# A Fourier mixing layer and an MLP on one core: the second half of a block's first w_out products is issued a step later

## The chip, the core and the metric

The kernel runs on one core of a Trainium2 chip. The core has a matrix engine (TensorE, "PE" in the profile, with its weight loads "PEld"), VectorE ("DVE"), ScalarE ("ACT"), GpSimd ("POOL") and SyncE ("SP", which here issues DMAs). The metric is the time of one execution on the device in microseconds, as the median of several runs.

## The reference

The input x is 8 sequences of 3008 tokens with 256 features. Each sequence is convolved along its tokens with a filter that is given by its spectrum, and the result goes through an MLP with a gated nonlinearity:

```
X = np.fft.rfft(x, axis=1)
F = (filt_r + 1j * filt_i)[None, :, :]
Y = X * F
y = np.fft.irfft(Y, n=x.shape[1], axis=1)      # 8 x 3008 x 256
h = y.reshape(24064, 256) @ w_in               # 24064 x 2048
g = h * (1.0 / (1.0 + np.exp(-beta * h)))
out = g @ w_out                                # 24064 x 256, float32
```

## The kernel before

The Fourier part is done as products with tables: 3008 = 47 * 64, so that a transform is a stage of 47 points (`s1`, L619), a stage of 64 points with the filter (`s23`, L641 to L670: a forward product, a complex multiplication with the filter on VectorE and GpSimd, an inverse product three units later), and a last stage of 47 points (`s4` through `last4`, L544). Between stages the data go through DRAM scratch to change their layout. The first sequence is done in a setup part of its own; the other seven are cut into small units, each with one or a few products and an evacuation, and a table `plan` says at which step of the MLP loop each unit is issued (`place`, L696).

The MLP loop (L812) takes 47 blocks of 512 tokens, and in each block 16 slices `fb` of 128 hidden features: 752 steps. In step s:

- two products of 512 columns (L825) give h for the slice in a PSUM tile `hps` (two buffers), and ScalarE turns it into `gT` (L834, Silu; w_out was divided by beta beforehand), in one of four buffers;
- then come the planned units of this step (L839). Their PSUM tiles are in `fpsum` (three buffers), and are emptied by VectorE or ScalarE;
- then, for the slice of two steps before (`LAG` is 2), four products of 256 columns (L860) add gT times w_out to the block's accumulators, one product for each 128 tokens (`tb`).

A block's accumulators are two PSUM tiles of two 128-token parts each, from `opsum`, which has three buffers (L83, L850). So of a new block's two tiles, the first finds the third buffer free, and the second takes the buffer that the old block's first tile leaves. At the end of a block (`fb` 15, L868) the two tiles are copied to SBUF one after the other by VectorE (`ost`, L109; in the first six blocks the first of the two by ScalarE, L107) and stored. In the last block each 128-token part has a tile of its own, from two pools.

The order on each engine is the order in which the Python code issues instructions: the kernel asks for a manual schedule, and the tile pools only add the waits. TensorE runs its products in this order, and a product that waits holds all behind it.

Of the kernel before, what the change touches and what calls it, by code (L numbers as in the profile page):

```python
# [9 lines left out]
P = 128  # L10
# [27 lines left out]
def kernel(  # L38
# [19 lines left out]
    NFB = FF // P  # L58
# [42 lines left out]
    wout_sb = wpool.tile([P, NFB, D], BF16, name="wout_sb", tag="wout_sb")  # L101
# [3 lines left out]
    def evac(dst, src, on_act, scale=None):  # L105
        if on_act:
            nc.scalar.activation(dst, src, ACT.Copy, scale=1.0 if scale is None else scale)  # L107
        elif scale is None:
            nc.vector.tensor_copy(dst, src)  # L109
        else:  # L110
            nc.vector.tensor_scalar_mul(dst, src, scale)  # L111
# [672 lines left out]
    def store(t0, tn, ost, eng=nc.sync):  # L784
        if t0 >= S:
            eng.dma_start(
                out[t0 : t0 + tn, :].rearrange("(c p) d -> p c d", p=P), ost[:, : tn // P, :]
            )
            return
        for tb in range(tn // P):  # L790
            c0 = t0 + tb * P
            c1 = c0 + P
            while c0 < c1:
                lo = (c0 - t0) % P
                if c0 >= S:
                    nc.sync.dma_start(out[c0:c1, :], ost[lo : lo + c1 - c0, tb, :])
                    break
                g, r = divmod(c0, CLS)
                n = min(c1 - c0, CLS - r)
                nc.sync.dma_start(  # L800
                    AP(
                        out.tensor,
                        out.offset + (r // JC * J + g * JC) * D,
                        [[J * D, n // JC], [D, JC], [1, D]],
                    ),
                    ost[lo : lo + n, tb, :],
                )
                c0 += n
# [3 lines left out]
    for s in range(len(steps) + LAG):  # L812
        if s < len(steps):
            i, fb = steps[s]
            t0 = i * TB
            tn = min(TB, TOK - t0)
            hps = hpsum.tile([P, TB], F32, name="hps", tag="hps")
            pos = t0
            while pos < t0 + tn:
                b, n0 = divmod(pos, S)  # L820
                ln = min(S - n0, t0 + tn - pos)
                if s == 0:
                    ln = min(ln, CLS - n0 % CLS)
                for dc in range(NDC):
                    nc.tensor.matmul(  # L825
                        hps[:, pos - t0 : pos - t0 + ln],
                        lhsT=win_sb[:, dc, fb * P : (fb + 1) * P],
                        rhs=ys[b][:, dc, n0 : n0 + ln],
                        start=(dc == 0),
                        stop=(dc == NDC - 1),  # L830
                    )
                pos += ln
            gT = gpool.tile([P, TB], BF16, name="gT", tag="gT")
            nc.scalar.activation(  # L834
                gT[:, :tn], hps[:, :tn], ACT.Silu, scale=beta_sb[:, fb : fb + 1]
            )
            blk[s] = gT
        if s in plan:
            for go in plan[s]:  # L839
                go()  # L840
        if s >= LAG:
            i, fb = steps[s - LAG]
            t0 = i * TB
            tn = min(TB, TOK - t0)
            nch = tn // P
            gT = blk.pop(s - LAG)

            last = i == NBLK - 1
            if fb == 0 and not last:
                acc = [opsum.tile([P, 2, D], F32, name="acc", tag="acc") for _ in range(2)]  # L850
            elif fb == 0:
                acc = [
                    (fpsum if h % 2 else opsum).tile(
                        [P, 1, D], F32, name="acc", tag="f" if h % 2 else "acc"
                    )
                    for h in range(nch)
                ]
            per = acc[0].shape[1]
            for tb in range(nch):
                nc.tensor.matmul(  # L860
                    acc[tb // per][:, tb % per, :],
                    lhsT=gT[:, tb * P : (tb + 1) * P],
                    rhs=wout_sb[:, fb, :],
                    start=(fb == 0 and tb % per == 0),
                    stop=(fb == NFB - 1),
                    skip_group_check=True,
                )
            if fb == NFB - 1:  # L868
                for h, a in enumerate(acc):
                    if h * per % 2 == 0:  # L870
                        ost = ostp.tile([P, 2, D], F32, name="ost", tag="ost")
                    c = h * per % 2
                    on_act = h == 0 and i < 6 or last and h % 2 == 0
                    evac(ost[:, c : c + per, :], a[:], on_act)
                    eng = nc.scalar if last and h >= 2 else nc.sync
                    store(t0 + h * per * P, per * P, ost[:, c : c + per, :], eng)
# [30 lines left out]
```

## Time and profile before

| | us |
|---|---|
| median of 7 runs | 789.67 (788.96 to 791.22) |
| the profiled execution | 791.28 |
| its span, first to last instruction | 789.5 |
| TensorE busy | 777.2 (98%) |
| ScalarE busy | 597.3 (76%) |
| VectorE busy | 394.1 (50%) |
| w_out products (L860), 3008 | 456.0 |
| w_in products (L825), 1730 | 448.2 |

The share of the TensorE clock that was granted is 0.998 over the span. A row of the order of time gives start, duration, engine, line, operation, the tiles written and read, their shapes, how many instructions were merged, and in brackets how long the engine sat idle before it and what ended that. Products of TensorE overlap: a 256-column product is shown with 273 ns, but the next one starts 109 ns after it, so that four in a row show 0.60 us. A wait between two of them can hide in a longer merged duration.

### The profile page before, as it was taken

What the parts mean: (1) busy time and instruction counts of PE and PEld (TensorE: products, weight loads), DVE (VectorE), ACT (ScalarE), POOL (GpSimd) and SP (SyncE); (2) the same over time, 40 slices, a digit from 0 to 9 for tenths busy, and PEclk for the clock granted to TensorE, in tenths of its full rate; (3) what the DMA queues carried; (4) which work ended last, traced back from release to release, by engine and by line L of the source; (5) the groups of instructions that cost most, each with busy time, mean ns of one, the idle gap of its engine ahead of it and who ended that gap; (6) DMA issues with size and microseconds to landing.
All of it is one profiled execution on the core that took longest, in us unless ns stands there. A gap on an engine that the chain in (4) does not pass through costs nothing.

```text
span 789.5 us, 15550 instructions
## 1 busy us (share of the span) xinstructions
PE 777.2 (98%) x6111; PEld 548.4 (69%) x6111; DVE 394.1 (50%) x645; ACT 597.3 (76%) x922; POOL 144.5 (18%) x143
## 2 busy tenths in 40 slices
PE   8989999999999999999999999999999999999998
PEld 5757667766777667876668766687667776776665
DVE  8837935746537464465534746367452761500101
ACT  6967886886678866788677876778767788677776
POOL 8522500430013200131002310024000340000000
PEclk9999999999999999999999999999999999999999
DMA  9978674516811178012860228412360214110101
GB/s 192 249 171 214 162 205 141 126 67 187 226 35 51 64 201 219 28 67 87 199 180 28 95 94 194 152 51 77 125 205 27 75 67 127 44 38 28 54 27 54
DMA packets 84185, 91.46 MB, mean 116 GB/s; under 512 B 4498, under 2 KB 74276, under 8 KB 83154
## 3 DMA queue, kind: packets, MB, share of 16 engines
q1 hardware_dynamic: 81008, 73.95, 30.3%
q0 software_dynamic: 2816, 16.26, 10.6%
q8 instruction: 48, 0.79, 0.4%
q10 hardware_dynamic: 288, 0.26, 0.1%
q14 instruction: 25, 0.20, 0.1%
HBM read 57.16 MB, written 46.66 MB: 131 GB/s over the span
## 4 chain that ended last, share of the span: by engine, by line
PE 91%; DVE 4%; DMA 2%; issue 2%; ACT 1%; POOL 0%; DVEq 0%; ACTq 0%; POOLq 0%
PE acc L860 41%; PE hps L825 40%; PE ps L619 3%; PE ps L544 3%; PE ps L641 2%; PE ps L667 2%; DVE ost L109 1%; DMA d<-a 1%; DVE qb_t L444 1%; DMA xg<-in_x_dram 1%; DVE pb_t L444 0%; DVE q_t L656 0%; DVE q_t L653 0%; DVE a_t L109 0%; PE pz L536 0%
## 5 line engine op out<-in xcount | busy, mean ns | idle before, releaser
L834 ACT ACTIVATE gT<-hps,beta_sb 128x512 bf16<-128x512 f32 x752 | 516.2, 687 | 176.8 <-PE hps L825 165.6
L860 PE MATMUL acc<-wout_sb,gT 128*128 128x256 bf16 x3008 | 456.0, 273 | 1.2 <-ACT ost L107 0.2
L825 PE MATMUL hps<-y,win_sb 128*128 128x512 bf16 (+8 forms) x1730 | 448.2, 351 | 0.3 <-ACT gT L834 0.3
L860 PEld LDWEIGHTS <-gT 128*128 128x128 bf16 x3008 | 285.7, 98 | 132.7 <-issue 4.6
L825 PEld LDWEIGHTS <-win_sb 128*128 128x128 bf16 x1730 | 165.0, 98 | 24.9 <-issue 0.6
L657 POOL TENSOR_TENSOR v_t<-p_t,q_t 128x512 bf16<-128x512 f32 x84 | 106.7, 1271 | 396.0 <-DVE q_t L656 393.1
L109 DVE COPY ost<-acc 128x512 f32<-128x512 f32 (+1 forms) x88 | 56.3, 678 | 193.6 <-PE acc L860 190.6
L109 DVE CAST a<-ps 96x512 bf16<-96x512 f32 x96 | 65.8, 686 | 90.4 <-PE ps L619 85.3
L111 DVE TENSOR_SCALAR y<-ps 128x376 bf16<-128x376 f32 (+1 forms) x119 | 64.5, 545 | 62.5 <-PE ps L544 62.4
L652 DVE TENSOR_TENSOR p_t<-ps,frr 128x512 f32<-128x512 f32 x84 | 58.1, 692 | 32.0 <-PE ps L641 29.3
L656 DVE TENSOR_TENSOR q_t<-ps,fri 64x512 f32<-64x512 f32 x84 | 58.3, 694 | 1.2
L653 DVE SCALAR_TENSOR_TENSOR q_t<-ps,fri 64x512 f32<-64x512 f32 x84 | 57.4, 684 | 1.1
L544 PEld LDWEIGHTS <-zz 96*128 96x128 bf16 x512 | 35.3, 97 | 31.0 <-issue 2.3
L107 ACT ACTIVATE z<-ps 128x512 bf16<-128x512 f32 x84 | 49.5, 590 | 0.8 <-PE ps L667 0.7
L619 PE MATMUL ps<-xg,t 94*96 94x512 bf16 x112 | 42.2, 382 | 0.0
L544 PE MATMUL ps<-t,zz 96*128 96x94 bf16 x448 | 36.7, 204 | 0.0
L667 PE MATMUL ps<-v_t,t 128*128 128x256 bf16 x168 | 32.1, 273 | 0.6 <-DVE q_t L656 0.6
L641 PE MATMUL ps<-a,t 128*128 128x256 bf16 x168 | 32.1, 273 | 0.0
L118 POOL DMA_DIRECT2D xg<-in_x_dram x22 | 12.1, 552 | 101.6 <-PE acc L860 97.7
L641 PEld LDWEIGHTS <-t 128*128 128x128 bf16 x168 | 15.8, 98 | 14.6
L619 PEld LDWEIGHTS <-t 94*96 94x96 bf16 x112 | 13.8, 123 | 12.1
L667 PEld LDWEIGHTS <-t 128*128 128x128 bf16 x168 | 15.4, 98 | 8.4 <-DVE q_t L656 1.4
(120 smaller groups left out, 195.6 us busy)
## 6 DMA issues: line engine op xcount, KB each, us to landing
out_dram<-ost SPq DMA_DIRECT2D x80, 256.0 KB, 2.1
d<-a SPq DMA_DIRECT2D x28, 384.0 KB, 3.7
a<-d SPq DMA_DIRECT2D x28, 384.0 KB, 5.2
d<-z SPq DMA_DIRECT2D x28, 384.0 KB, 2.3
zz<-d SPq DMA_DIRECT2D x28, 384.0 KB, 6.8
xg<-in_x_dram POOLq DMA_DIRECT2D x6, 1280.0 KB, 10.2
frr<-in_filt_r_dram SPq DMA_DIRECT2D x12, 256.0 KB, 6.8
out_dram<-ost SPq DMA_DIRECT2D x18, 128.0 KB, 2.4
```

What stands on the lines that cost most here:

```text
L109: nc.vector.tensor_copy(dst, src)
L111: nc.vector.tensor_scalar_mul(dst, src, scale)
L544: nc.tensor.matmul(ps[:, e, :NP], lhsT=zz[:, jj + e, dc * P : (dc + 1) * P], rhs=tab[:], start=True, stop=True,)
L619: nc.tensor.matmul(ps[:KP], lhsT=t1[:], rhs=s["x"][:, 2 * i : 2 * i + 2, :], start=True, stop=True)
L641: nc.tensor.matmul(ps[:, e, :], lhsT=t2[:, k0 + e, 3:5, :].rearrange("p c k -> p (c k)"), rhs=s["a2"][g][:, kk + e, :], start=True, stop=True,
L652: nc.vector.tensor_tensor(p_t[:], ps[:], frr[:, ks_, :], ALU.mult)
L656: nc.vector.tensor_tensor(q_t[:M], ps[M:P], fri[M:P, ks_, :], ALU.mult)
L657: nc.gpsimd.tensor_tensor(v_t[:], p_t[:], q_t[:], ALU.add)
L667: nc.tensor.matmul(ps[:, e, :], lhsT=t3[:, k0 + e, :], rhs=v_t[:, e, :], start=True, stop=True)
L825: nc.tensor.matmul(hps[:, pos - t0 : pos - t0 + ln], lhsT=win_sb[:, dc, fb * P : (fb + 1) * P], rhs=ys[b][:, dc, n0 : n0 + ln], start=(dc ...
L834: nc.scalar.activation(gT[:, :tn], hps[:, :tn], ACT.Silu, scale=beta_sb[:, fb : fb + 1])
L860: nc.tensor.matmul(acc[tb // per][:, tb % per, :], lhsT=gT[:, tb * P : (tb + 1) * P], rhs=wout_sb[:, fb, :], start=(fb == 0 and tb % per = ...
```

## The change

The loop over the four products at a step becomes a list of (gT, fb, tb). In a block's first step (`fb` 0) only the first half of the list (the 128-token parts 0 and 1, which go to the first tile) is issued; the second half is kept in `late`. In the next step (`fb` 1) the kept products are put into the middle of the list: parts 0 and 1 of slice 1, then parts 2 and 3 of slice 0, then parts 2 and 3 of slice 1. So at the next step TensorE runs the two L825 products, the planned units, and then six w_out products. All other steps are as before, and each sum is taken in the same order. In the new file the products stand at L867.

```
-            for tb in range(nch):
+
+
+            todo = [(gT, fb, tb) for tb in range(nch)]
+            if fb == 0:
+                todo, late = todo[: nch // 2], todo[nch // 2 :]
+            elif fb == 1:
+                todo[nch // 2 : nch // 2] = late
+            for g_, f_, tb in todo:
                 nc.tensor.matmul(
                     acc[tb // per][:, tb % per, :],
-                    lhsT=gT[:, tb * P : (tb + 1) * P],
-                    rhs=wout_sb[:, fb, :],
-                    start=(fb == 0 and tb % per == 0),
-                    stop=(fb == NFB - 1),
+                    lhsT=g_[:, tb * P : (tb + 1) * P],
+                    rhs=wout_sb[:, f_, :],
+                    start=(f_ == 0 and tb % per == 0),
+                    stop=(f_ == NFB - 1),
                     skip_group_check=True,
                 )
```

## The prediction

> **What bounds the kernel now.** I read the summary of busy time first, then the table of costliest groups, then the table of waits, then the order of time at the places where a block of 512 tokens ends.
>
> ```profile
> PE 777.2 (98%) x6111; PEld 548.4 (69%) x6111; DVE 394.1 (50%) x645; ACT 597.3 (76%) x922; POOL 144.5 (18%) x143
> ...
> L860 PE MATMUL acc<-wout_sb,gT 128*128 128x256 bf16 x3008 | 456.0, 273 | 1.2 <-ACT ost L107 0.2
> ```
>
> TensorE is the bound: 98% busy, and its chain of work is 91% of the span. The change removes no product, so it can only win time in which TensorE waits. By the group's row that is 1.2 us before the w_out products (L860). The table of waits shows more, on the weight loads of the same line:
>
> ```profile
> PEld L860 <- issue: 4.6, 20, 0.4
> ```
>
> Twenty waits, 4.6 us, at most 0.4 us each. The order of time says where they lie. This is block 8's first step:
>
> ```profile
> 180.13 1.27 DVE L109 COPY ost<-acc 128x512 f32<-128x512 f32 x2
> 180.20 0.38 PE L667 MATMUL ps<-v_t,t 128*128 128x256 bf16 x2
> 180.31 0.32 PEld L860 LDWEIGHTS <-gT 128*128 128x128 bf16 x3
> 180.42 0.83 PE L860 MATMUL acc<-wout_sb,gT 128*128 128x256 bf16 x4
> ...
> 180.87 0.10 PEld L860 LDWEIGHTS <-gT 128*128 128x128 bf16 x1 [0.24 <-issue]
> ```
>
> Four L860 products normally show 0.60 us and start 0.109 apart; here they take 0.83. The first two write the free third accumulator buffer. The third writes the buffer that held the old block's first half, which VectorE copies out until 180.13 + 0.68 = 180.81; it starts at 180.87. So 0.23 us is lost, inside what counts as busy.
>
> Here the Trainium skill must be weighed against the row. Perfetto Trace Analysis, "Identifying the Most-Contended Engine", says that TensorE's busy share is a bad measure of headroom, because pipelined products overlap. By the idle column (1.2 us) the change wins at most 0.15%, nothing measurable; by start-to-start times it may win four times that. The stretched 0.83 decides for the second.
>
> **What is removed.** I took the third product's start less the second's, less 0.109, at each of the 47 block starts. From 164 to 642 us the pattern repeats every six blocks: 0, 0.23, 0.28, 0.14, 0.07, 0, five times 0.72 = 3.60 us. The rest of the run has 0.14 once and 0.07 to 0.08 seven times: 0.67. Blocks 3, 4 and 5, where ScalarE copies the first half, have 0.15, 0.18 and 0.40: 0.72. Sum 5.0 us of waits for the old accumulator (the table's 4.6 plus pieces too short for it).
>
> **Where those products go.** In the new order the first step of a block has two L860 products instead of four; the next step's two L825 products follow (0.43 us), then a planned unit of the mixing, if that step has one, two of its own products (0.22), and then the two late ones. They come at least 0.65 us later than before, and the longest wait was 0.40. So all 5.0 us go. Nothing new is loaded or copied: still 64 products a block, each with its weight load; the queues of VectorE, ScalarE, GpSimd and SP keep their order, no DMA moves. The late products read the Silu result gT one step longer; four gT buffers rotate, and the Silu that overwrites one already waits for a later L825 product. If that cover were gone, ScalarE's 0.69 us Silu would slip, behind 0.2 to 0.4 us of its own slack.
>
> **What comes earlier.** Everything between is two products, 0.218 us, earlier against the other engines: L825 of the second step, and that step's unit.
>
> L825 needs a Silu of two steps before. At 180.87 ScalarE runs the first step's Silu, so the one needed ended before 180.46, while L825 would start at 180.42 + 0.22 = 180.64. No wait. The Silu behind it ends at 180.46 + 0.69 = 181.15, before the L825 after next.
>
> The unit is less safe. In twelve blocks (6, 7, 12, 13, 18, 19 and so on to 37, those with the 0 in the pattern) units of the third stage stand in the first and in the second step. Block 7:
>
> ```profile
> 164.38 0.69 ACT L834 ACTIVATE gT<-hps,beta_sb 128x512 bf16<-128x512 f32 x1 [0.18 <-PE hps L825]
> ...
> 164.55 0.60 PE L860 MATMUL acc<-wout_sb,gT 128*128 128x256 bf16 x4
> ...
> 164.96 0.59 ACT L107 ACTIVATE z<-ps 128x512 bf16<-128x512 f32 x1
> ...
> 165.42 0.38 PE L641 MATMUL ps<-a,t 128*128 128x256 bf16 x2
> 165.60 0.14 PEld L667 LDWEIGHTS <-t 128*128 128x128 bf16 x2
> 165.64 0.38 PE L667 MATMUL ps<-v_t,t 128*128 128x256 bf16 x2
> ```
>
> The second L667 unit takes the buffer that ScalarE empties into z: 164.96 + 0.59 = 165.55. Its weight load waits for that and starts at 165.60, just in time for a product at 165.64. Nothing ahead of z changes: Silu and z both depend on products issued before the moved ones. So z still ends at 165.55, while PE arrives at 165.64 - 0.218 = 165.42. What a late weight load costs is shown once in this trace, in block 6:
>
> ```profile
> 149.17 0.38 PE L641 MATMUL ps<-a,t 128*128 128x256 bf16 x2
> ...
> 149.55 0.11 PEld L667 LDWEIGHTS <-t 128*128 128x128 bf16 x2 [0.28 <-ACT z L107]
> 149.55 0.39 PE L667 MATMUL ps<-v_t,t 128*128 128x256 bf16 x2
> 149.67 0.42 PEld L860 LDWEIGHTS <-gT 128*128 128x128 bf16 x4
> 149.78 0.60 PE L860 MATMUL acc<-wout_sb,gT 128*128 128x256 bf16 x4
> ```
>
> The two L641 products should hand over at 149.17 + 0.22 = 149.39; L667 starts at 149.55, 4 ns after its load starts, and the next pair runs 10 ns late. So in block 7: 165.60 + 0.004 - 165.42 + 0.010 = 0.19 us. Eleven blocks times 0.19 is 2.1; block 6, which waits already, gets the whole 0.22 on top: 2.35 us in all.
>
> A rule of the skill speaks against the change just here. TensorE: Matmul & The Clock Gate, "Step-by-step: what each phase is for", lets the engine pull weight loads ahead, but "The MATMULs themselves stay in program order". If later products could pass the waiting one, the new waits would cost 0; by the rule they cost all of their 0.19. The row agrees with the rule: at 149.55 four ready L860 products stood behind L667 and none went ahead. I take the full cost.
>
> One more block: in block 3 the unit after is an L619 product at 98.50 whose buffer VectorE frees at 97.55 + 0.69 = 98.24 (q_t, L656). With the 0.15 us wait gone and two products fewer it would come at 98.13, and can come at 98.24 + 0.05: 0.15 us new, 0.03 of an old wait at 99.61 gone: 0.12.
>
> Lower bound of the new waits: 0, if the buffers were freed earlier, for which nothing speaks. Upper: 98 ns more at each of twelve places, if a product waits for its whole load (an L667 load's own duration): 1.2 us; the nearest row (4 ns at 149.55) is against it.
>
> **Sum.** 5.0 - 2.35 - 0.12 = 2.5 us, 0.32%. The profiled execution: span 789.5 us to 787.0; its own time 791.28 (1.8 outside the span) to 788.8. It stood 1.6 above the median of the runs, 789.67, so the median goes to 787.2.
>
> **Rivals.** (A) The new waits do not come: all 5.0 us won, 784.7 us. For it: the accumulator waits are certain, the L667 ones are shifted by arithmetic. Against: z's end at 165.55 leaves only 0.04 us.
>
> (B) The change doesn't do what it says: the late pair still waits, or every 0.218 us of advance is given back at the next unit, in nearly all blocks. Then 26 saved waits become other waits: 789.7. For it: after the wait is gone VectorE still does two copies (1.27 us) before its next unit. Against: the first units after the starts of blocks 8 and 9 have 2.4 us between their buffer's release and their start.
>
> (C) Slower: ScalarE becomes the bound in the twelve blocks. There a step costs PE 1.31 us (164.12 to 165.42), ScalarE a Silu and a z, at 0.58 + 0.72 between starts. In the shortened step PE asks again after 1.09. If z slips behind the next Silu by its 0.69 us, each place costs 0.19 + 0.69 = 0.88, together 10.6 us: 795.3. It decides above 5.0/12 = 0.42 us a place. For it: ScalarE has only 0.18 us idle there. Against: z stands before the next Silu in its queue, and that Silu's input comes after z has started.
>
> **How the numbers follow.** The sum as worked: 0.75. A: 0.08. B, or half of it: 0.12. C: 0.05. A measurement of this kernel tells about 0.2% (1.6 us) from no change; the seven runs lie 2.3 us apart. Faster by more means below 788.1: the sum's case less some bad luck (0.70) and A (0.08): 0.78. Within: 0.17. Slower: 0.05. The sum's own range is 786.3 to 788.3 (upper bound of the loads: gain 1.3); to hold eight in ten with half of A and of B it is 785.6 to 788.9.
>
> **What the new profile would show.** The first pair of a block's L860 products at 0.38 us and six after the next L825 (0.82 us), no stretched 0.83, no wait "PEld L860 <- issue" beyond the 55 us region. New: twelve waits of L667's loads for ScalarE's z (L107), near 0.19 us of PE time each, one of 0.38 in block 6. Wrong if these are absent (A), if L860 still waits for VectorE (B), or if L825 waits for Silu (C). Also outside my sum: at 55 us PE waits 2.0 us for a copy and the granted clock is 0.52 for 3.4 us, before the first changed wait; if its length differs between executions the median moves by about a microsecond.

## The result and the profile after

The changed kernel takes 786.86 us in the median (14 runs, 786.25 to 787.88), the kernel before 789.56 us (33 runs, 788.43 to 793.19). The ratio is 0.9964, with a 95% interval of 0.9956 to 0.9972: 2.7 us by the medians, 0.36% by the ratio, faster. The forecast was 787.2 us.

The page of the profiled execution, its first part and the row of the w_out products (L867 now):

```profile
span 784.7 us, 15550 instructions
...
PE 774.7 (99%) x6111; PEld 547.9 (70%) x6111; DVE 393.6 (50%) x645; ACT 595.1 (76%) x922; POOL 144.6 (18%) x143
...
L867 PE MATMUL acc<-wout_sb,gT 128*128 128x256 bf16 x3008 | 451.4, 272 | 0.0
```

The number of instructions is the same on every engine. The w_out products show 451.4 us busy where they showed 456.0: the 4.6 us less are mostly waits that had been counted as busy, in stretched merged products (the rest is the half clock near 55 us, told below). This is block 8's start in the order of time:

```profile
177.59 1.27 DVE L109 COPY ost<-acc 128x512 f32<-128x512 f32 x2
177.66 0.38 PE L667 MATMUL ps<-v_t,t 128*128 128x256 bf16 x2
177.77 0.21 PEld L867 LDWEIGHTS <-gT 128*128 128x128 bf16 x2
177.87 0.38 PE L867 MATMUL acc<-wout_sb,gT 128*128 128x256 bf16 x2
...
178.09 0.59 PE L825 MATMUL hps<-y,win_sb 128*128 128x512 bf16 x2
```

After the first pair the next L825 product starts 0.22 us later, the normal hand-over; the 0.83 us product group is gone, though VectorE's copy stands as late against TensorE as before. In the table of waits the twenty "PEld L860 <- issue" are gone (19 of them stood at block starts, one in the half clock near 55 us; a new one of 0.15 us stands in block 3, behind a product that waits there), and these rows are there (waiter, releaser, us in total, times, longest):

```profile
PEld L667 <- ACT z L107: 3.8, 12, 0.5
...
PEld L825 <- issue: 0.6, 1, 0.6
...
PE hps L825 <- ACT gT L834: 0.3, 1, 0.3
```

The kernel before has one wait of this kind, in block 6:

```profile
PEld L667 <- ACT z L107: 0.3, 1, 0.3
```

So eleven waits for ScalarE's z are new and block 6's is longer, and L825 has no waits beyond the single ones that stood before. Block 7's second step:

```profile
162.22 0.59 ACT L107 ACTIVATE z<-ps 128x512 bf16<-128x512 f32 x1
...
162.47 0.38 PE L641 MATMUL ps<-a,t 128*128 128x256 bf16 x2
162.73 0.69 ACT L834 ACTIVATE gT<-hps,beta_sb 128x512 bf16<-128x512 f32 x1
162.87 0.11 PEld L667 LDWEIGHTS <-t 128*128 128x128 bf16 x2 [0.30 <-ACT z L107]
162.87 0.39 PE L667 MATMUL ps<-v_t,t 128*128 128x256 bf16 x2
...
162.99 0.21 PEld L867 LDWEIGHTS <-gT 128*128 128x128 bf16 x2
163.10 0.27 PE L867 MATMUL acc<-wout_sb,gT 128*128 128x256 bf16 x1
```

L667 could have started at 162.47 + 0.22 = 162.69 and starts at 162.87. By start-to-start times it loses 0.186 us here and in each of the other ten blocks of this kind, and 0.385 in block 6, where 0.165 stood before.

The spans of the two profiled executions differ by 4.8 us, more than the medians. Past 60 us the difference is 2.4. The rest lies at 54 to 58 us, before the first changed wait: in both executions TensorE waits there for a PSUM buffer that ScalarE empties into `a`, and ScalarE waits for the DMA that copies an older `a` to DRAM. The kernel before:

```profile
54.21 0.59 ACT L107 ACTIVATE a<-ps 96x512 bf16<-96x512 f32 x1 [2.80 <-DMA d<-a]
...
54.86 0.33 PE L544 MATMUL ps<-t4b,zz 96*128 96x94 bf16 x4 [2.00 <-ACT a L107]
```

And after the change:

```profile
53.50 0.59 ACT L107 ACTIVATE a<-ps 96x512 bf16<-96x512 f32 x1 [2.08 <-DMA d<-a]
...
54.14 0.33 PE L544 MATMUL ps<-t4b,zz 96*128 96x94 bf16 x4 [1.29 <-ACT a L107]
```

By start-to-start times the wait is 2.17 us before and 1.45 after. Before, the granted clock was also halved behind it (the 0.52, third from the right, in this table of a stretch; the second row is the stretch after the change):

```profile
55.00:58.40 3.40, 3.40 (x22) 2.32 (x20) 0.78 (x2) 2.50 (x5) 0.00 (x0) 0.52 0.21 58
```

```profile
53.90:58.00 4.10, 3.86 (x39) 2.94 (x39) 1.95 (x4) 3.62 (x8) 0.00 (x0) 1.00 0.43 123
```

So the medians, not these two spans, measure the change.

### The profile page after: what moved, and what is told of

Its sections match the earlier page's. It is cut to its first block, busy times and chain, and to the rows that moved or that the text cites. A ratio compares the mean times of both kernels' runs of the same rounds, so it can differ in the third digit from the quotient of the medians.

```text
span 784.7 us, 15550 instructions
## 1 busy us (share of the span) xinstructions
PE 774.7 (99%) x6111; PEld 547.9 (70%) x6111; DVE 393.6 (50%) x645; ACT 595.1 (76%) x922; POOL 144.6 (18%) x143
## 4 chain that ended last, share of the span: by engine, by line
PE 94%; DVE 3%; issue 1%; DMA 1%; ACT 1%; DVEq 0%; ACTq 0%
PE acc L867 41%; PE hps L825 41%; PE ps L619 3%; PE ps L544 3%; PE ps L667 3%; PE ps L641 2%; PE pw L187 1%; DVE qb_t L444 1%; DMA d<-a 1%; DVE a_t L109 0%; ACT gT L834 0%; DVE pb_t L444 0%; DVE q_t L656 0%; DVE q_t L653 0%; PE pz L536 0%
## 5 line engine op out<-in xcount | busy, mean ns | idle before, releaser
L867 PE MATMUL acc<-wout_sb,gT 128*128 128x256 bf16 x3008 | 451.4, 272 | 0.0
L825 PE MATMUL hps<-y,win_sb 128*128 128x512 bf16 (+8 forms) x1730 | 447.7, 351 | 0.3 <-ACT gT L834 0.3
L867 PEld LDWEIGHTS <-gT 128*128 128x128 bf16 x3008 | 285.5, 98 | 127.4 <-ACT gT L834 0.2
L825 PEld LDWEIGHTS <-win_sb 128*128 128x128 bf16 x1730 | 165.0, 98 | 24.7 <-issue 0.6
L667 PE MATMUL ps<-v_t,t 128*128 128x256 bf16 x168 | 32.2, 273 | 1.1 <-DVE q_t L656 0.6
L641 PE MATMUL ps<-a,t 128*128 128x256 bf16 x168 | 32.1, 273 | 0.0
L641 PEld LDWEIGHTS <-t 128*128 128x128 bf16 x168 | 15.8, 98 | 14.6
L667 PEld LDWEIGHTS <-t 128*128 128x128 bf16 x168 | 15.1, 98 | 11.0 <-ACT z L107 3.8
```

Of the source, the lines that this page charges most:

```text
L641: nc.tensor.matmul(ps[:, e, :], lhsT=t2[:, k0 + e, 3:5, :].rearrange("p c k -> p (c k)"), rhs=s["a2"][g][:, kk + e, :], start=True, stop=True,
L667: nc.tensor.matmul(ps[:, e, :], lhsT=t3[:, k0 + e, :], rhs=v_t[:, e, :], start=True, stop=True)
L825: nc.tensor.matmul(hps[:, pos - t0 : pos - t0 + ln], lhsT=win_sb[:, dc, fb * P : (fb + 1) * P], rhs=ys[b][:, dc, n0 : n0 + ln], start=(dc ...
L867: nc.tensor.matmul(acc[tb // per][:, tb % per, :], lhsT=g_[:, tb * P : (tb + 1) * P], rhs=wout_sb[:, f_, :], start=(f_ == 0 and tb % per = ...
```

## The experiments

The theory: 5.0 us of waits for the old accumulator go, and about 2.4 us of new waits come, nearly all in the twelve blocks where a third-stage unit (one that contains L667's inverse product) stands in each of the first two steps. Rival 1: the gain is the shorter stretch near 55 us, through block 0's new order. Rival 2: TensorE makes up for the waits for z later, so that they cost nothing.

**The change in the twelve blocks alone** (no accumulator wait stood there):

```
-            if fb == 0:
+            if fb == 0 and i % 6 < 2 and 6 <= i < 38:
                 todo, late = todo[: nch // 2], todo[nch // 2 :]
-            elif fb == 1:
+            elif fb == 1 and i % 6 < 2 and 6 <= i < 38:
                 todo[nch // 2 : nch // 2] = late
```

> The second pair is held back only in the twelve blocks whose second step has a third-stage unit (6, 7, 12, 13, ... 36, 37), none of which had an accumulator wait. Theory (5.0 us of accumulator waits go, 2.3 us of waits for ScalarE's z come): only the cost is left, 11 x 0.186 + 0.22 = 2.3 us, 791.9 us, with twelve waits of L667's weight load for L107 in the trace. Rival 1 (the gain is the shorter stretch near 55 us, where the two profiled executions differ by 2.4 us, moved by block 0's new order): block 0 is as before, so 789.6 us. Rival 2 (the waits for z are made up later and cost nothing): 789.6 us.

Measured: 791.78 us (22 runs) against 789.69 for the kernel before, ratio 1.0026 (1.0017 to 1.0034). The table of waits of this run has both kinds:

```profile
PEld L867 <- issue: 4.3, 19, 0.4
...
PEld L667 <- ACT z L107: 3.8, 12, 0.5
```

This is the cost alone, 2.1 us. Rival 2 falls: the waits are not made up. Rival 1 is at 789.6 as well, and falls with it as an explanation of this run; the next run and the table at the end of this section speak of its gain.

**The change in all blocks but these** (the same two lines with `not (...)`):

> The second pair is held back in all blocks but those twelve. Theory: all 5.0 us of accumulator waits go, of the new waits only block 3's 0.14 us is left: 789.6 - 4.9 = 784.7 us. Rival 1 (the stretch near 55 us): block 0 has the new order, so as the change, 786.9 us. Rival 2 (waits for z cost nothing): as the change, 786.9 us.

Measured: 784.64 us (6 runs), ratio 0.9930 (0.9914 to 0.9946), 5.05 us faster than before. The waits of L667 for z are back to one:

```profile
PEld L667 <- ACT z L107: 0.3, 1, 0.3
```

Gain and cost, measured apart, are -5.05 and +2.09: together -2.96, where the whole change measured -2.7. Block 0 has the new order here and in the change, yet the two differ by 2.2 us, so Rival 1 cannot be the cause of that difference.

**The late pair ahead of the unit.** The pair is issued in the second step directly behind the L825 products, before the planned unit, so that the unit comes no earlier than it did:

```
+        if s >= LAG and steps[s - LAG][1] == 1:
+            w_out(late)
         if s in plan:
             for go in plan[s]:
                 go()
...
             if fb == 0:
                 todo, late = todo[: nch // 2], todo[nch // 2 :]
-            elif fb == 1:
-                todo[nch // 2 : nch // 2] = late
```

(`w_out` holds the loop over the products.)

> The second pair is held back in every block, but issued in the second step ahead of the planned unit instead of behind it, so that the unit comes no earlier than before. It is still 0.43 us (the two L825 products) later than before, and the longest accumulator wait was 0.40. Theory: 5.0 us won and no new wait: 784.6 us. Rival 1: 786.9 us. Rival 2: 786.9 us. A third possibility, that the pair waits again because 0.43 us is too short, would show as L860-type waits for VectorE or ScalarE and end between 784.6 and 786.9.

Measured: 784.00 us (6 runs, 783.52 to 784.88), ratio 0.9921 (0.9905 to 0.9937): the fastest kernel of this study. Block 7's second step in its order of time:

```profile
161.32 0.38 PE L815 MATMUL acc<-wout_sb,gT 128*128 128x256 bf16 x2
...
161.54 0.38 PE L641 MATMUL ps<-a,t 128*128 128x256 bf16 x2
...
161.72 0.14 PEld L667 LDWEIGHTS <-t 128*128 128x128 bf16 x2
161.76 0.38 PE L667 MATMUL ps<-v_t,t 128*128 128x256 bf16 x2
```

L667 follows L641 after the normal 0.22 us. Block 7 had no accumulator wait, but no row "PEld L815 <- issue" is left in the whole table of waits either, so 0.43 us of delay is enough for block 5's 0.40 too. Why it came 0.6 us lower than the sum is not settled; the sum lies at the interval's edge (0.9937 times 789.69 is 784.7). In its profiled execution the wait at 54 us was only 0.03 us, and behind that stretch it gained no more than the sum (table below).

**All four products held back**, which doubles the advance:

```
             if fb == 0:
-                todo, late = todo[: nch // 2], todo[nch // 2 :]
+                todo, late = [], todo
             elif fb == 1:
-                todo[nch // 2 : nch // 2] = late
+                todo = late[: nch // 2] + todo[: nch // 2] + late[nch // 2 :] + todo[nch // 2 :]
```

> All four products of a block's first step are held back to the second, which doubles the advance of what is issued between to 0.436 us. Theory: the twelve waits for z grow by 0.218 each to 0.40, 4.9 us with block 6; block 3's to 0.37; and where no unit stands in the first step (11 blocks) L825 comes 0.43 + 0.87 = 1.30 us after the L825 of two steps before, whose Silu ends after 0.216 + 0.48 + 0.69 = 1.39 and is seen 0.05 later: 0.13 us each, 1.5 us. Sum -5.0 + 4.9 + 0.3 + 1.5 = +1.7: 791.3 us. Rival 1: 786.9 us. Rival 2: 786.9 us, or 788.4 if only the L825 waits count.

Measured: 791.40 us (22 runs), ratio 1.0019 (1.0010 to 1.0028). Slower than before, though every accumulator wait is gone. The waits:

```profile
PEld L667 <- ACT z L107: 6.4, 12, 0.7
...
PEld L825 <- issue: 2.7, 10, 0.6
```

By start-to-start times L667 loses 0.405 us in eleven blocks and 0.602 in block 6, which is the 0.186 of the change plus the 0.218 of two more products. And L825 waits for the Silu of two steps before in 13 blocks, about 0.13 us each; the expectation had counted 11. This is the order of time at such a place, the start of block 40: four L825 products merged, 1.16 us instead of 0.435 + 0.59 = 1.03.

```profile
687.16 1.16 PE L825 MATMUL hps<-y,win_sb 128*128 128x512 bf16 x4
688.15 1.03 PE L867 MATMUL acc<-wout_sb,gT 128*128 128x256 bf16 x8
```

**The units moved away.** The change, with third-stage units never in two steps that follow each other:

```
                 at += (2 - at) % NFB
+            if clear and n and at - last_at < 2:
+                at = last_at + 2
```

> The change, with the third-stage units never in two steps that follow each other: a unit that would stand in a block's second step goes to its third. Theory: the twelve waits for z go, because z has a whole step more; all 5.0 us of accumulator waits are won, block 3's new 0.14 us stays, and block 6's old wait of 0.17 goes: 789.7 - 5.0 = 784.7 us. If the wait for z is not a matter of where the unit stands but follows the advance wherever the next unit is, the trace shows L667 waiting for L107 in the third step, and the time stays at 786.9 us.

Measured: 784.64 us (6 runs) against 789.54, ratio 0.9937 (0.9921 to 0.9953). No wait of L667 for z is left in its table, and nothing appears in the third step. The control, the kernel before with the same two lines:

> The kernel before, with the same spacing of the units and nothing else: the control for the run beside it. Theory: these units wait for nothing before the change (block 6's 0.17 us apart), so 789.5 us, and the accumulator waits stay in the trace as they were. If the spacing itself is worth something, it shows here, and is to be taken off the other run's gain.

Measured: 789.89 us (14 runs), ratio 1.0003 (0.9992 to 1.0014), with the accumulator waits as they were (19 at block starts; the twentieth row of the kernel before was the one in the half clock):

```profile
PEld L862 <- issue: 4.3, 19, 0.4
```

So the spacing is worth nothing by itself, and it is the neighbouring unit that the change runs into.

**Behind the stretch at 55 us.** Each trace (one execution each) can also be measured without that stretch, from the start of step 36's Silu (near 80 us in the kernel before) to the start of the last TensorE product:

| kernel | this part, us | less the kernel before | medians, less the kernel before |
|---|---|---|---|
| before | 705.2 | | |
| the change | 702.8 | -2.4 | -2.7 |
| twelve blocks alone | 707.6 | +2.4 | +2.1 |
| all blocks but these | 700.4 | -4.8 | -5.05 |
| late pair ahead of the unit | 700.7 | -4.5 | -5.7 |
| all four held back | 707.2 | +2.1 | +1.7 |
| units moved away | 700.2 | -5.0 | -4.9 |
| spacing alone | 705.2 | +0.1 | +0.35 |

Gains and costs lie in this part, which the stretch at 55 us does not enter, so Rival 1 is not their cause. Where the medians differ from this part, by 0.3 us for the change, the stretches ahead of it or the other executions must account for it; how was not tried. In the late-pair run 0.5 us of the 5.0 was lost again near 80 us, where an L667 product waits longer for VectorE's q_t (1.06 us against 0.56 before).

## Why the prediction was right

**The bound.** That the idle column understates the waits was right and decided the sign of anything measurable: by the 1.2 us of the idle column, less the new waits, the change would have been a loss. The 5.0 us from start-to-start times were measured as 5.05 with all costs but block 3's 0.14 left out (the ratio's interval reaches from 4.3 to 6.8 us), and as 4.8 in the trace behind 55 us. So the step holds that weighed the Trainium skill's page Perfetto Trace Analysis, "Identifying the Most-Contended Engine", against the stretched 0.83 us. One of the table's twenty waits, 0.21 us at 55.34, belonged to the half clock and not to an accumulator; the sum of 5.0 does not contain it.

**The removal.** All waits at the 47 block starts are gone; 0.65 us of delay was enough, and 0.43 is too.

**The new waits.** The step by which z still ends when it did and TensorE arrives 0.218 us earlier was right to a few nanoseconds: 0.186 us measured per block and 0.010 on the next pair, 0.19 predicted. (Block 6 was not the only late load to learn from: the kernel before has three more of L667, which wait for VectorE's q_t; the one at 95.94 also has its product in the same hundredth of a microsecond.) Block 6 got 0.22 on top, as written. Block 3 got 0.167 less an old 0.026, 0.14 where 0.12 was written. Products behind the waiting one did not pass it: the next L867 product starts at 163.10, after L667 at 162.87. This agrees with the rule that the prediction took from the Trainium skill (TensorE: Matmul & The Clock Gate, "Step-by-step: what each phase is for"), and the row that spoke for it was the one at 149.55.

**The sum.** -5.0 + 11 x 0.196 + 0.22 + 0.14 = -2.5; measured -2.7 by the medians, -2.4 past 60 us in the profiles. What was wrong was only the profiled span: 787.0 was written and 784.7 came, because the stretch at 55 us was 2.4 us shorter, and the prediction had named this stretch as outside its sum.

**The rivals.** A, no new waits: 784.7 us, which the change did not reach. That is the time of the kernel once another edit takes the waits away (784.64 with the units moved). B, every advance given back at the next unit: this happened only where that unit's buffer was just in time, in the twelve blocks and block 3. (B speaks of 26 saved waits; the prediction's own list has 31.) C, ScalarE as the bound from 0.42 us a place on: the change cost 0.196 a place. With all four products held back a place cost 0.41, which nearly used up the gain, and L825's waits (13 times 0.13 us) came on top. That agrees with C's break-even, which is only 5.0 us over twelve places; C's mechanism, a z that slips behind a Silu, was seen in no run.

## What to carry to other kernels

When work is moved out of the way of a late buffer, whatever moves up into its place arrives earlier at its own buffers: look at each of them for the slack it has, in nanoseconds, at every place where the pattern repeats. A place with no wait in the profile may be just in time. If the delayed work can go ahead of the next sensitive unit and still be late enough (0.43 us here for a wait of 0.40), the gain costs nothing: 784.0 us instead of 786.9. And on a saturated engine, measure waits by start-to-start times, since merged durations hide them.

## What the runs showed of the hardware

The wait at 54 us, for a buffer whose copy to DRAM is under way, differed between the profiled executions: 2.17 us and half clock behind it (before), 1.45 (the change), 1.14 to 1.70 in three others, 0 to 0.15 in three. It differs for programs that are the same up to there: 2.17 and 1.20 us for the kernel before and the change in the twelve blocks alone, 1.45 and 0.15 for the change and the change in all blocks but these. So a single profiled span can be off by nearly as much as the change is worth. Over the runs shared by the first four experiments, 6 of 43 executions of the kernel before had a mean granted clock of 0.998 or less, and their median was 791.9 us where that of the others was 789.6. The profiled execution with the half clock also has 0.998; that the stretch at 55 us is where the other slower executions lost their time was not seen. Whether the longer wait is what lowers the clock was not tried.
